# The last row's second layer norm from moments, in an adaLN, cached attention and token-mixing kernel

## The chip, the cores and the metric

The kernel runs on one core of a Trainium2 chip. The metric is the device time of one execution in microseconds (us); a run's time is given as the median of several executions. Each core has five engines with instruction queues of their own, each worked off in order: TensorE (PE in the profile, its weight loads PEld), VectorE (DVE), ScalarE (ACT), GpSimd (POOL) and SyncE (SP, which here issues nearly all DMAs).

## The reference

Four rows (batch B = 4, one token each, D = 512 channels), all arrays fp32. Cut to what matters:

```python
mod = (silu(c) @ w_mod).reshape(4, 6, 1, 512)       # sa, ca, ga, sb, cb, gb
h = layernorm(x) * (1 + ca) + sa
x = x + ga * attention(h, k_cache, v_cache, wq, wo) # 32 query heads, 8 kv heads, 4096 cached positions, head size 128
h = layernorm(x) * (1 + cb) + sb
# token mixing: a second layer norm of h, then one number per channel through an MLP of width 1792
n = layernorm(h)
u = gelu_tanh(n * w1 + b1)                          # (channel, 1792)
y = u @ w2 + b2                                     # one number per channel
out = x + gb * y
```

Each layer norm uses the variance over 512 channels with eps = 1e-5. The key and value caches are 2 MB for each of the 32 (row, kv head) pairs and kind, 128 MB in all; with the weights 157 MB are read.

## The kernel before

The 32 (row, head) pairs are numbered 0 to 31, eight of one row after another. Keys and values come in 4 MB loads (`load_pair`) into a ring of three slots, all on SyncE's queue. For each pair: `scores` (TensorE), the maximum over a row (`row_max`, `turn_max`, `col_max`, `spread_max`, `copy_max`), `expo` (ScalarE), `turn` (a transpose on VectorE), `values` (TensorE), `copy_v`, `pick`, `copy_o`, `project` (times wo) and `add_up`. The first 24 pairs run in a loop over `i`; the last eight follow a plan written out by hand, `PLAN`, a string of steps in which a letter names the operation and a number the pair: `V29` is `copy_v(29)`, `P28` is `add_up(28)`. The scheduler is manual: each engine executes its instructions in the order in which the program issues them.

While the pairs of row b + 1 run, the class `Mixer` does row b's modulation and mixing in small steps: `expand` (`x`, VectorE, two of the 14 chunks of the MLP width: u = hb * wr + b1 over all 512 channels), `gelu` (`g`, ScalarE, on such a chunk pair), `consume` (`c`, TensorE, contraction with w2 into the PSUM tile `py`). Row 2 is thus mixed during row 3's pairs, by the plan. Its last chunk pair is expanded into spare room of the slot that holds modulation 5 (`load_wm5`, step `LW`), and its last two pairs are contracted in the tail (`c c` in the last line of the plan), with `gather_up` (`zc`) copying `py` to SBUF on VectorE and folding it.

The channel layout: a [128, 128] tile holds row b of chunk c on the eight partitions from 32 * c + 8 * b, so 512 channels are four groups of partitions by 128 columns, and statistics over a row need a matmul across partitions.

Row 3, the last, has no pairs to hide behind. Its chain in the tail, after the last projection has filled `pgx[:, 4]` in PSUM and its mean was worked out ahead (`tally`, `mu`):

- `zs` (L741): ScalarE squares (x + mu) and sums along the columns; `zq` (L737): a matmul sums over the partitions.
- `za` (`centre`, L410): VectorE, a = (x + mu) * (1 + cb); `zx` (L747): a copy of x to `XK`.
- `zm` (`adaln_last`, L413): ScalarE's root sd (L416); h1 = sb * sd + a (L417), that is the modulated row times sd; terms that carry eps through the next norm (L419); its statistics `stats` (L378, L380).
- `T3` (L733): loads ScalarE's gelu tables with an activation of one element.
- `zb0`, `zb1` (`bcast`, L427): h1 spread over all partitions, two chunks of 128 channels each, into PSUM.
- `zv` (L479): the matmul that gathers the statistics; `zn` (`affine`): the aggregate (L396), hb = h1 - mean over all partitions in two halves on ScalarE (L436), the power -0.5 on GpSimd (`root`, L100) and wr = w1 * y (L437).
- `zw0` (L209): a quarter of modulation 5; then `finish` (L552): 14 chunks of expand, gelu and contract for the last row, closing and output.

Of the kernel before, what the change touches and what calls it, by code (L numbers as in the profile page):

```python
# [28 lines left out]
def adaln_decode(ctx: ExitStack, tc: tile.TileContext, small, x, wmod, wq, kk, kv, vv, wo, out):  # L29
# [47 lines left out]
    nc.gpsimd.memset(epsr[:, :, 2:3], EPS * 64)  # L77
    eps9 = cst.tile([P, 3], F32, name="eps9")
    nc.gpsimd.memset(eps9, 0.0)
    nc.gpsimd.memset(eps9[:, 0:1], 1e-20)  # L80
    nc.gpsimd.memset(eps9[:, 2:3], EPS * D)
    g32 = cst.tile([P, 32], F32, name="g32")
    dv.tensor_reduce(g32, ident.rearrange("p (c r) -> p r c", c=4), axis=AX.X, op=OP.add)
    eight = g32.rearrange("p (r x) -> p r x", x=8)[:, :, 0]
    sel4 = g32.rearrange("p (j r e) -> p j r e", j=4, e=2)[:, :, :, 0]
# [7 lines left out]
    prep = cst.tile([P, 4, P], F32, name="prep")  # L93
    osb = cst.tile([P, B, P], F32, name="osb")
    sT8 = cst.tile([P, 4, B, 8], F32, name="sT8")
# [63 lines left out]
    def slots():  # L159
        return ring.tile([P, 2, SK], F32, name="kv", tag="kv")  # L160
# [29 lines left out]
    def load_wm5():  # L190
        t = slots().rearrange("p s (k n) -> p (s k) n", n=D)
        nc.sync.dma_start(t[:, 0:4], wmod[2][:, 1])
        WM[5] = t[:, 0:4]
        return t[:, 4:6]

# [176 lines left out]

    XK = cst.tile([P, B, P], F32, name="xk")
    ZK = cst.tile([P, B - 1, P], F32, name="zk")
# [32 lines left out]

    def centre(x, mu):
        a = wk.tile([P, P], F32, name="a")
        dv.scalar_tensor_tensor(a, x, mu, prep[:, 3], op0=OP.add, op1=OP.mult)  # L410
        return a

    def adaln_last(b, pst, a):  # L413
        r = cst.tile([P, 1], F32, name="sd")
        h1 = wk.tile([P, P], F32, name="h1")
        nc.scalar.activation(r, pst, AF.Sqrt, bias=epsc, scale=1.0 / D)  # L416
        dv.scalar_tensor_tensor(h1, prep[:, 2], r, a, op0=OP.mult, op1=OP.add)  # L417
        pst = ps_m.tile([P, 27], F32, name="pst", tag="m")
        dv.tensor_scalar(pst[:, 24:27], eps9, r, r, op0=OP.mult, op1=OP.mult)  # L419
        return h1, stats(h1, b), pst  # L420

    def bcast(h1, b, pb=None, cs=range(4)):
# [26 lines left out]

    def contract_wide(py, u, js):  # L450
        for e, j in enumerate(js):
            q = j % 4
            mm(py[32 * q:32 * q + 32, :], w2[:, j:j + 1].to_broadcast([P, 32]), u[:, e, :],  # L453
               start=(j < 4), stop=(j >= NF - 4))

    class Mixer:
# [20 lines left out]

        def gather_more(self):
            mm(self.pst[:, 0:24], ones, self.st.rearrange("p a b -> p (a b)"), start=True, stop=True)  # L479
            self.st = self.pst  # L480

        def modulate(self):
            if self.b < B - 1:
                self.h1, self.st = adaln(self.b, self.st)
            else:
                self.h1, self.st, self.pst = adaln_last(self.b, self.st, self.a)

# [25 lines left out]
        def consume(self, most=9):  # L513
            if self.py is None:
                self.py = ps_e.tile([P, D if self.wide else P], F32, name="py", tag="e")
            for u, js in self.done[:most]:
                (contract_wide if self.wide else contract)(self.py, u, js)
            del self.done[:most]

        def gather_up(self):  # L520
            yw = wk.tile([P, D], F32, name="yw", tag="yw", bufs=1)
            dv.tensor_copy(yw, self.py)
            self.py = fold_groups(ps_e, yw, "e")

        def close(self):
# [25 lines left out]

    def finish(b, pg, py, hb, wr):  # L552
        uu = ring.tile([P, 16, D], F32, name="uu", tag="kv")
        for js in ((0,), (1,), (2, 3, 4), (5, 6, 7), (8, 9, 10), (11, 12), (13,)):
            j = js[0]
            if j < 2:
                nc.scalar.activation(uu[:, j], hb, AF.Gelu_apprx_tanh, bias=b1[:, j:j + 1], scale=wr[:, j:j + 1])
                u = uu[:, j:j + 1]
            else:
                u = uu[:, j:j + len(js)]  # L560
                expand(u, hb, wr, js)
                nc.scalar.activation(u, u, AF.Gelu_apprx_tanh)  # L562
            contract(py, u, js)
            if j == 1:
                modmm(pg, 5, (1, 2, 3))
        mix.close()
        dv.tensor_mul(osb[:, :B - 1], ZK, pg.unsqueeze(1).to_broadcast([P, B - 1, P]))
        dv.tensor_add(osb[:, :B - 1], osb[:, :B - 1], XK[:, :B - 1])
# [3 lines left out]
        dv.scalar_tensor_tensor(gx, gbl, b2, XK[:, b], op0=OP.mult, op1=OP.add)  # L572
# [23 lines left out]
    both = cst.tile([P, 2 * REP], F32, name="both")  # L596
    mu = cst.tile([P, 1], F32, name="mu")

    def tally_up():
# [18 lines left out]
    for i in range(NS - HKV):  # L618
# [30 lines left out]
        if i == 2:  # L649
            for t in range(2, 5):  # L650
                pm = mod(t)
                dst = prep[:, {2: 1, 3: 2, 4: 3}[t]]
                if t == 4:
                    dv.tensor_scalar(dst, pm, 1.0, None, op0=OP.add)
                else:
                    nc.scalar.activation(dst, pm, AF.Copy)
        if i == NS - HKV - 2:
            gate = spread_gate()

    mix, row = Mixer(B - 2), Mixer(B - 1)
    pve = pgx = pc = ep = spare = slot = None
    gates = list(range(2 * REP))
# [7 lines left out]
    LV28 L28 a27 g X30 t29.1 t29.0 l29 L29 s31 A27 LV29 b30 p27 x B30 S31 c c m31 e30 P27 X31 v28.0 f LT LV30  # L672
    b31 v28.1 B31 f e31 LV31 l30 V28 L30 t30.1 l31 L31 a28 t31.1 A28 p28 v29.0 v29.1 t30.0 f P28 V29 v30.0 a29
    v30.1 A29 LW p29 f v30.2 v30.3 t31.0 P29 g V30 Y y a30 A30 p30 E x v31.0 f v31.1 v31.2 v31.3 V31 z31 a31 I A31 j p31
    g T2 zs za zx zq c c zm zb0 T3 zv zb1 zw0 zn zc
    """
# [3 lines left out]
    MIX = {"F": mix.fold, "R": mix.residual, "G": mix.gather, "M": mix.modulate, "H": mix.gather, "Q": mix.spread,  # L680
           "N": mix.normalise, "g": mix.gelu, "c": lambda: mix.consume(1), "zc": mix.gather_up, "zv": row.gather_more,
           "zg": row.gather,
           "zm": row.modulate, "zn": lambda: row.normalise(cst.tile([P, 1], F32, name="yl"))}
    for step in PLAN.split():
# [25 lines left out]
        elif op == "LW":  # L710
            spare = load_wm5()
        elif op == "x":
            mix.expand(spare if mix.n == 6 else None)
        elif op == "f":
# [15 lines left out]
        elif step == "T2":  # L730
            nc.scalar.activation(tab, ones[0:1, 0:1], AF.Sqrt)
        elif step == "T3":
            nc.scalar.activation(tab, neg1, AF.Gelu_apprx_tanh)  # L733
        elif op == "zq":
            ph = ps_s.tile([P, 8, P], F32, name="ph3", tag="s")
            row.st = ph[:, 2, 0:1]
            mm(row.st, g32[:, 8 * (B - 1):8 * (B - 1) + 1].to_broadcast([P, P]), sq, start=True, stop=True)  # L737
        elif op == "zs":
            sq = cst.tile([P, 1], F32, name="sq")
            flat = wk.tile([P, P], F32, name="flat")  # L740
            nc.scalar.activation(flat, pgx[:, 4], AF.Square, bias=mu, accum_out=sq)  # L741
        elif op == "j":
            tally_up()
        elif op == "za":
            row.a = centre(pgx[:, 4], mu)
        elif op == "zx":
            dv.tensor_copy(XK[:, B - 1], pgx[:, 4])  # L747
        elif op == "zw":
            modmm(pgx[:, 0], 5, (0,))
        elif op == "zb":  # L750
            if i:
                py = ps_v.tile([P, 4, P], F32, name="py3", tag="pv")
            row.spread(py[:, 2:4] if i else ph[:, 4:6], (2 * i, 2 * i + 1))
    finish(B - 1, pgx[:, 0], py[:, 0], row.hb, row.wr)

# [33 lines left out]
```

## Time and profile before

| what | value |
| --- | --- |
| device time, median of 3 runs | 386.49 us (386.45 to 386.63) |
| span of the profiled execution, first to last instruction | 384.7 us |
| TensorE busy | 298.7 us (78%) |
| VectorE busy | 198.2 us (52%) |
| ScalarE busy | 112.2 us (29%) |
| GpSimd busy | 7.7 us (2%) |
| loads | 157.3 MB, q1 95.4% of the 16 DMA engines' span |

The profile gives the span of its execution; its own device time beside that is not listed, and the span lies 1.8 us under the median of the runs. A row of the timeline reads: start in us from the span's start, duration in us, engine, line, operation, output <- inputs, shapes, count, and in brackets how long the engine had been idle and what ended that.

### The profile page before, as it was taken

How to read it: one execution, taken by the hardware profiler on the slowest of the kernel's cores; microseconds unless marked ns; L12 is line 12 of the kernel's file. 1: busy time of each engine (PE TensorE's matmuls, PEld its weight loads, DVE VectorE, ACT ScalarE, POOL GpSimd, SP SyncE). 2: the span in 40 equal slices, each digit the busy share in tenths (PEclk: the TensorE clock that was granted, in tenths of full speed). 3: DMA queues.
4: the chain of work that ended last, by engine and by line, in shares of the span. 5: the costliest groups of instructions: out<-in, count | busy, mean ns of one | idle time of the engine just before them, and what ended most of it. 6: DMA issues, size and time to landing. Idle time of an engine off the chain costs nothing.

```text
span 384.7 us, 5604 instructions
## 1 busy us (share of the span) xinstructions
PE 298.7 (78%) x2380; PEld 117.2 (30%) x2380; DVE 198.2 (52%) x407; ACT 112.2 (29%) x144; POOL 7.7 (2%) x33
## 2 busy tenths in 40 slices
PE   0856777866966949979877878788888887999984
PEld 0112122311323313334322222342222343333653
DVE  1130251620451424664866545557665567778757
ACT  1001111121110110212567311124575105657276
POOL 1100000000000000000000000000000000000000
PEclk9989555985695685998999998999999999999999
DMA  8999999999999999999999999999999999999930
GB/s 331 433 433 436 411 453 433 409 432 436 423 441 433 434 436 436 434 436 431 429 425 433 428 433 434 429 433 431 429 434 436 434 436 432 424 417 423 418 122 3
DMA packets 7409, 157.69 MB, mean 410 GB/s; under 512 B 964, under 2 KB 1236, under 8 KB 1496
## 3 DMA queue, kind: packets, MB, share of 16 engines
q1 hardware_dynamic: 7376, 157.33, 95.4%
q8 instruction: 18, 0.29, 0.3%
q14 instruction: 7, 0.06, 0.0%
q10 hardware_dynamic: 8, 0.00, 0.0%
HBM read 157.32 MB, written 0.01 MB: 409 GB/s over the span
## 4 chain that ended last, share of the span: by engine, by line
DMA 60%; PE 29%; DVE 7%; ACT 2%; issue 1%; POOL 0%; SPq 0%; POOLq 0%; DVEq 0%
DMA kv<-in_kv 58%; PE s L231 8%; PE pv L291 7%; PE s L122 2%; PE qs L138 2%; DVE m L236 2%; DVE p L267 2%; DMA sm<-in_small 2%; PE pa L343 2%; PE pt L328 2%; ACT uu L562 1%; PE pb L251 1%; PE pve L303 1%; PE pm L240 1%; PE pgx L348 1%
## 5 line engine op out<-in xcount | busy, mean ns | idle before, releaser
L231 PE MATMUL s<-kv,QT 128*32 128x512 f32 x512 | 75.2, 714 | 38.9 <-DMA kv<-in_kv 37.0
L236 DVE TENSOR_REDUCE m<-s 128x1 f32<-128x1024 f32 x32 | 39.2, 1224 | 96.0 <-PE s L231 95.9
L261 ACT ACTIVATE p<-s,nm 128x1024 f32<-128x1024 f32 x32 | 35.7, 1115 | 180.6 <-DVE nm L256 180.5
L291 PE MATMUL pv<-kv,p 128*32 128x512 f32 x464 | 69.8, 670 | 0.7 <-DMA kv<-in_kv 0.7
L231 PEld LDWEIGHTS s<-kv,QT 128*32 128x32 f32 x512 | 15.8, 123 | 84.0 <-DMA kv<-in_kv 52.5
L328 PEld LDWEIGHTS pt<-g,po 128*128 128x128 f32 x236 | 31.1, 205 | 27.2 <-issue 19.9
L343 PE MATMUL pa<-wo,oT 128*32 128x512 f32 x240 | 34.6, 648 | 4.6 <-DVE oT L335 4.4
L328 PE MATMUL pt<-g,po 128*128 128x4 f32 (+2 forms) x236 | 33.9, 267 | 1.5 <-DVE po L314 1.0
L267 DVE STREAM_TRANSPOSE p<-p 128x1024 f32<-128x1024 f32 x25 | 30.9, 1234 | 0.0
L314 DVE COPY po<-pv 128x512 f32<-128x512 f32 x29 | 20.0, 688 | 16.8 <-PE pv L291 16.7
L245 DVE TENSOR_REDUCE mx<-pm 1x128 f32<-1x512 f32 x32 | 21.3, 669 | 1.1 <-PE pm L240 1.1
L442 DVE TENSOR_SCALAR u<-hb,wr,sm 128x512 f32<-128x512 f32 x40 | 19.9, 541 | 1.9 <-POOL wr L437 1.0
L506 ACT ACTIVATE u<-u 128x1024 f32<-128x1024 f32 x20 | 20.4, 1051 | 1.5 <-DVE u L442 1.4
L361 DVE TENSOR_TENSOR acc<-acc,pa 128x512 f32<-128x512 f32 x26 | 17.8, 686 | 4.3 <-PE pa L343 4.2
L261 ACT ACT_TABLE_LOAD x11 | 14.1, 1283 | 20.3 <-DVE nm L256 20.2
L251 PEld LDWEIGHTS pb<-neg,mx 1*128 1x128 f32 x64 | 10.4, 202 | 28.2 <-DVE mx L245 26.5
L122 PE MATMUL s<-wm,sT 128*4 128x512 f32 x16 | 9.1, 732 | 10.6 <-DVE sT L108 10.6
L506 ACT ACT_TABLE_LOAD x13 | 16.7, 1283 | 0.2
L291 PEld LDWEIGHTS pv<-kv,p 128*32 128x32 f32 x464 | 13.4, 146 | 7.2 <-issue 3.1
L240 PE MATMUL pm<-ident,m 128*1 128x128 f32 x32 | 9.3, 289 | 7.4 <-DVE m L236 3.5
L251 PE MATMUL pb<-neg,mx 1*128 1x1 f32 x64 | 13.1, 271 | 2.1 <-DVE mx L245 2.1
L453 PE MATMUL py<-u,sm 128*32 128x512 f32 x80 | 14.4, 616 | 0.0
(158 smaller groups left out, 214.7 us busy)
## 6 DMA issues: line engine op xcount, KB each, us to landing
kv<-in_kv SPq DMA_DIRECT2D x28, 4096.0 KB, 21.9
wq<-in_wq SPq DMA_DIRECT2D x2, 4096.0 KB, 16.3
wo<-in_wo SPq DMA_DIRECT2D x4, 2048.0 KB
kv<-in_kv SPq DMA_DIRECT2D x4, 2048.0 KB, 20.3
wm<-in_wmod SPq DMA_DIRECT2D x2, 2048.0 KB, 14.8
kv<-in_kk SPq DMA_DIRECT2D x1, 4096.0 KB
kv<-in_vv SPq DMA_DIRECT2D x3, 1024.0 KB
wm<-in_wmod SPq DMA_DIRECT2D x1, 1024.0 KB
```

Source lines behind the costliest of these rows:

```text
L231: mm(s[32 * c:32 * c + 32, n * 512:(n + 1) * 512], QT[:, b, h, :], KT[i][:, (n * 4 + c) * 512:(n * 4 + c + 1) * 512], start=True, stop=True)
L236: dv.tensor_reduce(M[i], S[i], axis=AX.X, op=OP.max)
L245: dv.tensor_reduce(mx, M[i].rearrange("o (c r) -> o r c", c=4).unsqueeze(1).to_broadcast([1, 4, 32, 4]), axis=AX.X, op=OP.max)
L251: mm(pb, M[i].rearrange("o c r -> o (c r)"), neg1, start=True, stop=True)
L261: nc.scalar.activation(p, S[i], AF.Exp, bias=M.pop(i), accum_out=l)
L267: dv.transpose(PL[i][0], PL[i][0])
L291: mm(PV[i][32 * q:32 * q + 32, :], pT[:, 128 * k:128 * k + 128:4], VT[i][:, 4 * k:4 * k + 4, :].rearrange("p j d -> p (j d)"), start=(k < ...
L314: dv.tensor_copy(PV[i], pv)
L328: mm(pt, po[:, c * DH:(c + 1) * DH], sel.unsqueeze(1).to_broadcast([P, m, REP]), start=(c == 0), stop=(c == n - 1))
L343: mm(pa[32 * g:32 * g + 32, :], oT[:, g:g + 1].to_broadcast([P, 32]), wo_t[h][:, g, :], start=True, stop=True)
L442: dv.tensor_scalar(u[:, e, :], hb, wr[:, j:j + 1], b1[:, j:j + 1], op0=OP.mult, op1=OP.add)
L506: nc.scalar.activation(u, u, AF.Gelu_apprx_tanh)
```

## The change

The last row's second variance is no longer taken from statistics of h1 but worked out from moments. With the shift sb centred beforehand (`spread_shift`, in the loop after pair 5, gives `spart` = sb minus its mean and sb's variance plus eps in `smv`), h1 = spart * sd + al, and the variance over the row times sd squared is E[al^2] + sd * E[2 al spart] + sd^2 * (var(sb) + eps) - (E[al])^2. The four sums along columns go into `mom`: ScalarE squares give the columns 0 and 2, VectorE's accumulators the columns 1 and 3; matmuls with constant columns 1/D and -1/D (`mid`, `nmid`) sum over partitions, each into a PSUM tile of its own (`row`, the tile of `first_moment`, and `ph[:, 0]`). Two small factors run on GpSimd (`kk1`), two on VectorE (`vv1`). The upper half of hb is written by VectorE, the lower by ScalarE. The copy of x to `XK` is gone; `gx` reads x from PSUM.

Row 2: the last `x` and its gelu, and the gelu before it, move ahead of `V29`; there `lift` (`zy`) copies the ten contracted chunks from `py` to SBUF on ScalarE. In the tail `fold_rest` (`zc`) folds that copy and contracts the last four chunks in narrow form. The output tile `osb` comes from the ring of `u` tiles.

```diff
-    eps9 = ...                                   # three memsets on GpSimd
+    mid = cst.tile([P, 1], F32, name="mid")
+    nc.gpsimd.tensor_scalar(mid, g32[:, 8 * (B - 1):8 * (B - 1) + 1], 1.0 / D, None, op0=OP.mult)
+    nmid = ...                                   # the same with -1.0 / D
...
-    def contract_wide(py, u, js):
+    def contract_wide(py, u, js, last):
...
-               start=(j < 4), stop=(j >= NF - 4))
+               start=(j < 4), stop=(last - 4 < j))
...
+        def lift(self):
+            self.yw = up.tile([P, 2, D], F32, name="u")[:, 0]
+            nc.scalar.activation(self.yw, self.py, AF.Copy)
+
+        def fold_rest(self):
+            py = ps_e.tile([P, P], F32, name="pc", tag="e")
+            for c in range(4):
+                mm(py[32 * c:32 * c + 32, :], g32, self.yw[:, c * P:(c + 1) * P], start=True, stop=False)
+            for u, js in self.done:
+                for e, j in enumerate(js):
+                    for c in range(4):
+                        mm(py[32 * c:32 * c + 32, :], w2[:, j:j + 1].to_broadcast([P, 32]),
+                           u[:, e, c * P:(c + 1) * P], start=False, stop=(j == NF - 1))
+            self.py = py
...
+    def spread_shift():                          # called in the loop where i == 5
+        psb = ps_m.tile([P, 4, P], F32, name="psb", tag="m")
+        for c in range(4):
+            e = 32 * c + 8 * (B - 1)
+            mm(psb[:, c, :], ident[:, e:e + 1].to_broadcast([P, P]), prep[:, 2], start=True, stop=True)
+        psb = psb.rearrange("p c n -> p (c n)")
+        st = wk.tile([P, 6], F32, name="st")
+        dv.bn_stats(st, psb)
+        dv.bn_aggr(smv, st)
+        dv.tensor_scalar(spart, prep[:, 2], smv[:, 0:1], None, op0=OP.subtract)
+        dv.tensor_scalar(smv[:, 1:2], smv[:, 1:2], EPS, None, op0=OP.add)
...
+    def last_rows(x):                            # za
+        al = wk.tile([P, P], F32, name="a")
+        flat = wk.tile([P, P], F32, name="flat")
+        dv.scalar_tensor_tensor(al, x, mu, prep[:, 3], op0=OP.add, op1=OP.mult, accum_out=mom[:, 1:2])
+        dv.tensor_tensor_reduce(flat, al, spart, 2.0, 0.0, OP.mult, OP.add, mom[:, 3:4])
+        return al
+    def squares(x, col, **kw):                   # zs (x + mu, column 0), zp (al, column 2)
+        flat = wk.tile([P, P], F32, name="sqr", tag="h1")
+        nc.scalar.activation(flat, x, AF.Square, accum_out=mom[:, col:col + 1], **kw)
+    def means(cols, dst=None, mid=mid):          # zq, zl, zv
+        if dst is None:
+            dst = ps_m.tile([P, 1], F32, name="pmo", tag="m")
+        mm(dst, mid.to_broadcast([P, P]), mom[:, cols], start=True, stop=True)
+        return dst
+    def first_root(g):                           # zk
+        nc.scalar.activation(sd, g, AF.Sqrt, bias=epsc)
+        nc.gpsimd.tensor_scalar(kk1[:, 0:1], sd, sd, smv[:, 1:2], op0=OP.mult, op1=OP.mult)
+    def modulate(al):                            # zh
+        h1 = wk.tile([P, P], F32, name="h1")
+        dv.scalar_tensor_tensor(h1, spart, sd, al, op0=OP.mult, op1=OP.add)
+        return h1
+    def first_moment(g):                         # zl
+        dv.tensor_copy(momc, g)
+        nc.gpsimd.tensor_scalar(kk1[:, 1:2], momc, momc, kk1[:, 0:1], op0=OP.mult, op1=OP.subtract)
+    def second_moments(g):                       # zm
+        dv.tensor_sub(vv1[:, 0:1], g[:, 0:1], kk1[:, 1:2])
+        dv.scalar_tensor_tensor(vv1[:, 1:2], g[:, 1:2], sd, vv1[:, 0:1], op0=OP.mult, op1=OP.add)
+    def affine_last(lo, hi):                     # zn
+        ...
+        root(vv1[:, 1:2], P, y)
+        nc.scalar.activation(hb[:, 0:D // 2], lo, AF.Identity, bias=momc)
+        dv.tensor_scalar(hb[:, D // 2:], hi, momc, None, op0=OP.add)
+        nc.gpsimd.tensor_tensor(wr, w1, y.to_broadcast([P, NF]), op=OP.mult)
...
-    f P28 V29 v30.0 a29
-    v30.1 A29 LW p29 f v30.2 v30.3 t31.0 P29 g V30 Y y a30 A30 p30 E x v31.0 f ... j p31
-    g T2 zs za zx zq c c zm zb0 T3 zv zb1 zw0 zn zc
+    f P28 g x g zy V29 v30.0 a29
+    v30.1 A29 LW p29 f v30.2 v30.3 t31.0 P29 V30 Y y a30 A30 p30 E v31.0 f ... j p31
+    T2 zs za zp zq zk T3 zl zh zv zm zb0 zb1 zn zw0 zc
```

More of the change, by code (lines that the diff above doesn't have):

```diff
@@ L656, in adaln_decode @@
                     nc.scalar.activation(dst, pm, AF.Copy)
+        if i == 5:
+            spread_shift()
         if i == NS - HKV - 2:
             gate = spread_gate()
-    mix, row = Mixer(B - 2), Mixer(B - 1)
-    pve = pgx = pc = ep = spare = slot = None
+    mix = Mixer(B - 2)
+    pve = pgx = pc = ep = slot = None
     gates = list(range(2 * REP))
@@ L680, in adaln_decode @@
     MIX = {"F": mix.fold, "R": mix.residual, "G": mix.gather, "M": mix.modulate, "H": mix.gather, "Q": mix.spread,
-           "N": mix.normalise, "g": mix.gelu, "c": lambda: mix.consume(1), "zc": mix.gather_up, "zv": row.gather_more,
-           "zg": row.gather,
-           "zm": row.modulate, "zn": lambda: row.normalise(cst.tile([P, 1], F32, name="yl"))}
+           "N": mix.normalise, "g": mix.gelu, "c": lambda: mix.consume(1), "zy": mix.lift, "zc": mix.fold_rest, }
     for step in PLAN.split():
@@ L710, in adaln_decode @@
         elif op == "LW":
-            spare = load_wm5()
+            load_wm5()
         elif op == "x":
-            mix.expand(spare if mix.n == 6 else None)
+            mix.expand()
         elif op == "f":
@@ L733, in adaln_decode @@
             nc.scalar.activation(tab, neg1, AF.Gelu_apprx_tanh)
-        elif op == "zq":
-            ph = ps_s.tile([P, 8, P], F32, name="ph3", tag="s")
[L736 to L741, printed above, removed]
+        elif op == "zs":
+            squares(pgx[:, 4], 0, bias=mu)
+        elif op == "za":
+            al = last_rows(pgx[:, 4])
+        elif op == "zp":
+            squares(al, 2)
+        elif op == "zq":
+            row = means(slice(0, 1))
+        elif op == "zk":
+            first_root(row[:, 0:1])
+        elif op == "zh":
+            h1 = modulate(al)
+        elif op == "zl":
+            first_moment(means(slice(1, 2), None, nmid))
+        elif op == "zv":
+            ph = ps_s.tile([P, 8, P], F32, name="ph3", tag="s")
+            means(slice(2, 4), ph[:, 0, 0:2])
+        elif op == "zn":
+            hb, wr = affine_last(*(t.rearrange("p c n -> p (c n)") for t in (ph[:, 4:6], py[:, 2:4])))
+        elif op == "zm":
+            second_moments(ph[:, 0, 0:2])
         elif op == "j":
             tally_up()
[L744 to L747, printed above, removed]
         elif op == "zw":
```

67 lines of the change are left out of this document (30 added, 37 removed).

## The prediction

> **What bounds the kernel now.** I read the chain that ended last first, then busy times by stretch, then the timeline of the last 25 us, engine by engine. The chain, as shares of the span by engine:
>
> ```profile
> DMA 60%; PE 29%; DVE 7%; ACT 2%; issue 1%; POOL 0%; SPq 0%; POOLq 0%; DVEq 0%
> ```
>
> Busy time by stretch near the end, columns named in its second line:
>
> ```profile
> core 0 of [0], span 384.7 us
> core 0: us, PE busy (x) PEld busy (x) DVE busy (x) ACT busy (x) POOL busy (x), PEclk, DMA share, GB/s
> 364.00:368.00 4.00, 3.64 (x98) 3.11 (x98) 2.64 (x10) 1.69 (x2) 0.00 (x0) 1.00 0.88 352
> 368.00:372.00 4.00, 3.42 (x59) 2.18 (x59) 1.91 (x10) 2.43 (x6) 0.00 (x0) 1.00 0.19 80
> 372.00:376.00 4.00, 2.89 (x54) 2.00 (x57) 3.06 (x8) 3.59 (x7) 0.76 (x2) 1.00 0.01 4
> ```
>
> The loads bound the span up to about 367 us. The last values are what TensorE waits for:
>
> ```profile
> 367.23 0.14 PEld L303 LDWEIGHTS pve<-kv,p 128*32 128x32 f32 x4 [0.17 <-DMA kv<-in_vv]
> ```
>
> Then 17.4 us of tail run with hardly a load: the last row's residual, statistics, modulation, second statistics, fourteen gelus, output. Most of the change lies there. The in-order queues of ScalarE, VectorE, TensorE and GpSimd, from the square of the last row to the gelus:
>
> ```profile
> 369.94 0.37 ACT L741 ACTIVATE flat<-pgx,mu 128x128 f32<-128x128 f32 x1 [1.07 <-PE pgx L348]
> 370.20 0.19 ACT L741 ACTIVATION_READ_ACCUMULATOR flat<-pgx,mu 128x1 f32 x1
> 370.87 0.26 ACT L416 ACTIVATE sd<-ph,epsc 128x1 f32<-128x1 f32 x1 [0.47 <-PE ph L737]
> 371.15 1.28 ACT L733 ACT_TABLE_LOAD   x1
> 372.44 0.20 ACT L733 ACTIVATE tab<-neg 1x1 f32<-1x1 f32 x1
> 372.96 0.47 ACT L436 ACTIVATE hb<-ph,mv 128x256 f32<-128x256 f32 x1 [0.31 <-DVE mv L396]
> 373.33 0.47 ACT L436 ACTIVATE hb<-py,mv 128x256 f32<-128x256 f32 x1
> 373.88 1.52 ACT L557 ACTIVATE uu<-hb,sm,wr 128x512 f32<-128x512 f32 x2
> 375.38 1.48 ACT L562 ACTIVATE uu<-uu 128x1536 f32<-128x1536 f32 x1
> ```
>
> ```profile
> 370.43 0.35 DVE L410 SCALAR_TENSOR_TENSOR a<-pgx,mu,prep 128x128 f32<-128x128 f32 x1 [0.77 <-ACT flat L741]
> 370.70 0.28 DVE L747 COPY xk<-pgx 128x128 f32<-128x128 f32 x1
> 371.16 0.35 DVE L417 SCALAR_TENSOR_TENSOR h<-prep,sd,a 128x128 f32<-128x128 f32 x1 [0.18 <-ACT sd L416]
> 371.43 0.28 DVE L419 TENSOR_SCALAR pst<-eps,sd 128x3 f32<-128x3 f32 x1
> 371.62 0.28 DVE L378 BATCH_NORM_STATS2 st<-h 128x6 f32<-128x128 f32 x1
> 371.94 0.18 DVE L380 TENSOR_TENSOR stm<-st,ident 128x24 f32<-128x24 f32 x1
> 372.64 0.28 DVE L396 BATCH_NORM_AGGREGATE mv<-pst 128x2 f32<-128x27 f32 x1 [0.52 <-PE pst L479]
> 372.84 0.63 DVE L522 COPY yw<-py 128x512 f32<-128x512 f32 x1
> 373.89 2.37 DVE L442 TENSOR_SCALAR uu<-hb,wr,sm 128x512 f32<-128x512 f32 x5 [0.42 <-POOL wr L437]
> ```
>
> ```profile
> 371.23 0.60 PE L453 MATMUL py<-kv,sm 128*32 128x512 f32 x2
> 371.75 0.71 PE L427 MATMUL ph<-h,ident 128*128 128x128 f32 x4
> 372.30 0.30 PE L479 MATMUL pst<-stm,ones 128*128 128x24 f32 x2
> 372.45 0.69 PE L427 MATMUL py<-h,ident 128*128 128x128 f32 x4
> ```
>
> ```profile
> 373.00 0.55 POOL L100 TENSOR_TENSOR yl<-mv,half 128x1 f32<-128x1 f32 x1 [54.02 <-DVE mv L396]
> 373.63 0.21 POOL L437 TENSOR_TENSOR wr<-w1n,yl 128x14 f32<-128x14 f32 x1
> ```
>
> From 373.88 ScalarE runs gelu on gelu without a gap, and the end follows at a fixed distance. So the question is when the first gelu of the last row starts. Now wr, ready at 373.84, starts it, after the chain square, root, h1, statistics, gather matmul, aggregate, power, product.
>
> **The change, part by part.**
>
> *Prologue.* Three memsets leave GpSimd and two 128x1 multiplies join. Between L437's 0.21 and L100's 0.55 each, they delay what follows on that queue by 0.1 to 0.8 us. I take 0, because the load queue is busy with the query weights then; without that cover it is this amount.
>
> *spread_shift after pair 5.* Eight passes like L427's (1.2 us at this clock), a 512-wide PSUM read (0.63 by L522), an aggregate (0.28) and two small operations: about 2.5 us, in front of the next pair. The cover:
>
> ```profile
> 143.25 1.08 PE L231 MATMUL s<-kv,QT 128*32 128x512 f32 x4 [5.20 <-DMA kv<-in_kv]
> ```
>
> TensorE waits 5.2 us for a load shortly after. Cost 0.
>
> *Row 2.* Its last expand, two gelus and a new copy to SBUF (lift) move ahead of copy V29 in the order. On VectorE that is between these two:
>
> ```profile
> 358.65 0.69 DVE L361 TENSOR_TENSOR acc<-acc,pa 128x512 f32<-128x512 f32 x1
> 360.40 0.29 DVE L314 COPY po<-pvn 128x128 f32<-128x128 f32 x1 [1.06 <-PE pvn L303]
> ```
>
> Two expands take 0.95 (five take 2.37) and fit the 1.06 idle, with some 0.1 to spare. Behind V29 wait pick, copy_o and project of pair 29 and the last values; the only later slack on that path is the 0.17 at the last load. The gelus and the lift run on ScalarE, which nothing else needs then. No DMA moves past another. In the tail the eight wide matmuls of 371.23 go, and fold_rest brings 8 + 32 narrow passes after the first part of modulation 5. Twelve such passes took this long:
>
> ```profile
> 364.71 0.53 PE L348 MATMUL pgx<-wo,both 128*32 128x128 f32 x12 [0.25 <-DVE both L335]
> ```
>
> So 40 take about 1.5 us. They begin near 373.4 and end near 374.9. The first contraction could start 0.8 us after the first gelu (L557: two in 1.52), at 374.4; it loses 0.5, which does not reach the end, since TensorE has only 8 + 8 + 24 more passes before the three-wide gelu ends near 376.6. Cost 0.
>
> *XK copy and output.* The 0.28 copy leaves VectorE, which then waited for the root anyway; gx reads PSUM, as L410 does in 0.35, the same as from SBUF. 0.
>
> *The tail, worked out.* Square and its accumulator end at 370.39, as now. The centring waits for the square now (0.77 <-ACT), and I keep that: 370.43 to 370.78. The new square of al comes ahead of the root on ScalarE. It has no per-partition bias; its price is this copy's:
>
> ```profile
> 36.12 0.28 ACT L155 ACTIVATE prep<-px 128x128 f32<-128x128 f32 x1
> ```
>
> 370.82 plus 0.28, and the accumulator's read overlapping 0.1: to 371.19. Root: 371.21 to 371.47, so 0.34 later than now. Behind it three ways run to the gelu:
> - ScalarE: table load to 372.77, warm-up to 372.97, lower half 0.47: 373.44, gelu at 373.5.
> - VectorE: h1 371.50 to 371.85. Then all eight broadcast passes without the statistics in between: now from 371.83 (end of L453) to 373.14, less 0.15 for L479, is 1.16, so 371.89 to 373.05. Upper half on VectorE: 0.28 at 128 columns and 0.63 at 512 give 0.40; with a scalar pointer I take 0.46, near ScalarE's 0.47. 373.09 to 373.55, gelu at **373.59**.
> - GpSimd: first factor from 371.55 (0.08 after its input, as at 373.00), second, then two VectorE operations of about 0.2 with hand-overs, power 0.55, product 0.21. A 128x1 multiply by pointer scalars has no row; its bounds are 0.21 (L437) and 0.55 (L100). I take 0.25, nearest to L437, also a multiply: factors done 372.13, variance 372.53, power 372.61 to 373.16, product 373.24 to 373.45, gelu at 373.5. At 0.21 it is 373.4, at 0.55 374.1.
>
> The latest decides: 373.59 against 373.88, a gain of **0.29 us**. Span 384.7 becomes 384.4. Only the span of the profiled execution is shown; the runs' median, 386.49, lies 1.8 above it, and I take the gain from the median: **386.2**.
>
> [...] GpSimd and VectorE overlap here now, in the same order of things as the first factor and h1 will:
>
> ```profile
> 314.57 0.38 DVE L404 SCALAR_TENSOR_TENSOR a<-xk,mv,prep 128x128 f32<-128x128 f32 x1
> ```
> ```profile
> 314.61 0.55 POOL L100 TENSOR_TENSOR ye<-mv,half 128x1 f32<-128x1 f32 x1 [55.49 <-DVE mv L396]
> ```
>
> GpSimd's power takes 0.55 beside a VectorE operation with two SBUF inputs, as it does at 373.00 beside one without, and VectorE 0.38 instead of 0.35. So I charge nothing. [...]
>
> **The rivals.**
> 1. *GpSimd decides.* Each 0.1 on a factor costs 0.2 on that way. Above 0.3 each it is the latest; above 0.44 each the kernel is slower than before: 386.7 at the 0.55 bound. Past 0.2% needs 0.83 each. For: pointer scalars are unpriced, and the power takes 0.55 for one column. Against: fourteen columns multiplied in 0.21. [...]
> 2. *The centring does not wait for the square*, since it is a different program: al at 369.95, its square behind the first one, root as now; the three ways start 0.34 earlier: 385.9. Against: both still read one PSUM tile, and L410 waits for ScalarE though it needs nothing of it.
> 3. *Slower: TensorE's granted clock falls* when the eight wide matmuls leave the middle of the tail. At half clock the 1.16 of broadcast passes becomes 2.3, and the gelu starts at 374.75: 387.4. It decides if the clock drops before 371.9. Against: TensorE is dense up to 370, and kept 1.00 in the stretch 372 to 376 with 2.89 of 4 us busy; about 2.5 remain.
> 4. *The tail's start moves.* The load stream lasts 365 us, and 0.2% of it is as much as all else; or the expand runs into V29. 385.4 to 386.9. Against: no byte and no load's order changes, and the runs shown lie within 0.18.
>
> **How the numbers follow.** What a measurement of this kernel can tell from no change is about 0.2%, 0.77 us. Forecast (VectorE's or ScalarE's way last, 386.0 to 386.45) 0.60; rival 1 (386.4 to 386.8) 0.15, of which 0.02 past the bound; rival 2 0.08, of which 0.02 below 385.72; rival 3 0.04; rival 4 0.13, of which 0.06 faster and 0.02 slower. Faster 0.08, slower 0.08, same 0.84. The range reaches down to 385.8, under rival 2's time, and up to 386.8, over rival 1's upper bound.
>
> **What would show it.** First gelu 0.2 to 0.4 us earlier against the end of the last values; the root some 0.3 later than now; the last three rows before the gelu those of VectorE's half; factors of 0.2 to 0.3 on GpSimd; broadcast passes in one block of 1.2 us; row 2's last gelus before 362 us and V29 not later than 360.5; a TensorE wait for a load at the last values as now. Wrong would be: factors over 0.44, a centring beside the square, a granted clock under 1.00 before 374, or last values off 367.2 by more than 0.3.

## The result, and the profile after

| | before | after |
| --- | --- | --- |
| device time, median of 5 runs | 386.49 us (386.41 to 386.63) | 388.55 us (388.26 to 389.75) |
| ratio, 95% interval | | 1.0057 (1.0045 to 1.0069) |
| span of the profiled execution | 384.7 | 387.9 (its own time: 389.75) |
| square of the last row to its first gelu | 3.94 | 4.87 |

The change costs 2.06 us where 0.29 us of gain was forecast. The profiled execution after is the slowest of the five; four have spans of 386.5 to 386.7. In it 2.26 us are lost ahead of the tail: the square starts at 372.20 instead of 369.94. TensorE's granted clock (third figure from the end) is low in one stretch there, first after, then before:

```profile
280.00:290.00 10.00, 9.77 (x45) 3.63 (x45) 3.88 (x6) 3.42 (x4) 0.00 (x0) 0.54 0.99 429
```
```profile
280.00:290.00 10.00, 7.96 (x65) 2.98 (x69) 6.51 (x12) 7.43 (x9) 0.00 (x0) 1.00 0.99 426
```

Another execution of the same kernel (again, below) has 1.00 in this stretch and the square at 369.96, so that part belongs to this one execution. The lag opens there: ScalarE's exponentials of one pair start at 277.63 here and 278.04 in again, those of the next pair at 290.39 and 286.35. That the clock caused it is not shown. From the first gelu to the end of the span it is 10.8 in both kernels. So the loss that both traced executions share lies between the square and the first gelu.

The timeline of after, from the square to the gelu:

```profile
372.20 0.37 ACT L623 ACTIVATE sqr<-pgx,mu 128x128 f32<-128x128 f32 x1 [6.16 <-PE pgx L346]
373.08 0.31 ACT L623 ACTIVATE sqr<-a 128x128 f32<-128x128 f32 x1 [0.43 <-DVE a L617]
373.39 0.24 ACT L632 ACTIVATE sd<-pmo,epsc 128x1 f32<-128x1 f32 x1
373.54 0.38 PE L628 MATMUL ph<-mom,mid 128*128 128x2 f32 x2
373.67 0.35 DVE L637 SCALAR_TENSOR_TENSOR h<-spart,sd,a 128x128 f32<-128x128 f32 x1
373.74 0.49 POOL L633 TENSOR_SCALAR kk<-sd,smv 128x1 f32<-128x1 f32 x1 [50.88 <-DVE momc L641]
374.33 0.39 POOL L642 TENSOR_SCALAR kk<-momc,kk 128x1 f32<-128x1 f32 x1
374.76 0.16 DVE L645 TENSOR_TENSOR vv<-ph,kk 128x1 f32<-128x1 f32 x1 [0.74 <-POOL kk L642]
374.95 0.22 DVE L646 SCALAR_TENSOR_TENSOR vv<-ph,sd,vv 128x1 f32<-128x1 f32 x1
375.22 0.71 PE L411 MATMUL ph<-h,ident 128*128 128x128 f32 x4 [1.30 <-DVE vv L646]
375.77 0.61 PE L411 MATMUL py<-h,ident 128*128 128x128 f32 x4
375.97 0.47 ACT L653 ACTIVATE hb<-ph,momc 128x256 f32<-128x256 f32 x1 [0.83 <-PE ph L411]
376.42 0.48 DVE L654 TENSOR_SCALAR hb<-py,momc 128x256 f32<-128x256 f32 x1 [1.25 <-PE py L411]
377.07 0.81 ACT L552 ACTIVATE uu<-hb,sm,wr 128x512 f32<-128x512 f32 x1 [0.62 <-DVE hb L654]
```

h1 (L637) is done at 374.02, but its broadcast (L411) starts at 375.22. The bracket names VectorE's second operation on the moments (L646), a value that the broadcast does not use. It does share the tile: the second moments lie in `ph[:, 0]`, which is not a tile of their own, since the lower half of the broadcast goes to `ph[:, 4:6]`. The operation ahead of L646 (L645) in turn waits for the two factors on GpSimd, 0.49 and 0.39.

Busy time by stretch, after:

```profile
core 0: us, PE busy (x) PEld busy (x) DVE busy (x) ACT busy (x) POOL busy (x), PEclk, DMA share, GB/s
374.00:375.20 1.20, 0.00 (x0) 0.00 (x0) 0.39 (x3) 1.13 (x2) 0.62 (x2) 1.00 0.00 0
375.20:376.20 1.00, 0.98 (x8) 0.97 (x8) 0.00 (x0) 0.23 (x1) 0.77 (x2) 1.00 0.00 0
376.20:378.20 2.00, 2.00 (x38) 1.88 (x40) 1.59 (x4) 1.38 (x3) 0.00 (x0) 0.54 0.05 12
```

TensorE (first pair of numbers) does nothing for 1.2 us, and about 1 us later its granted clock falls to half (0.54 as the mean of that stretch). That was too late to hurt the broadcast here.

### The profile page after: what moved, and what is told of

It reads as the page before. It is cut to its first block, busy times and chain, and to the rows that moved or that the text cites. A ratio compares the mean times of both kernels' runs of the same rounds, so it can differ in the third digit from the quotient of the medians.

```text
span 387.9 us, 5682 instructions
## 1 busy us (share of the span) xinstructions
PE 308.7 (80%) x2414; PEld 123.7 (32%) x2414; DVE 199.2 (51%) x412; ACT 112.6 (29%) x146; POOL 8.8 (2%) x34
## 4 chain that ended last, share of the span: by engine, by line
DMA 44%; PE 41%; DVE 11%; ACT 2%; POOL 1%; issue 1%; SPq 0%; ACTq 0%; POOLq 0%; DVEq 0%
DMA kv<-in_kv 42%; PE s L229 10%; PE pv L289 10%; PE pa L341 4%; PE pt L326 3%; DVE m L234 3%; DVE p L265 2%; PE s L121 2%; PE qs L137 2%; DMA sm<-in_small 2%; PE pb L249 2%; ACT uu L557 1%; PE py L437 1%; PE pm L238 1%; PE pve L301 1%
## 5 line engine op out<-in xcount | busy, mean ns | idle before, releaser
L229 PE MATMUL s<-kv,QT 128*32 128x512 f32 x512 | 76.8, 727 | 33.9 <-DMA kv<-in_kv 32.1
L289 PE MATMUL pv<-kv,p 128*32 128x512 f32 x464 | 72.5, 695 | 0.0
L326 PEld LDWEIGHTS pt<-g,po 128*128 128x128 f32 x236 | 32.8, 214 | 28.4 <-issue 18.7
L341 PE MATMUL pa<-wo,oT 128*32 128x512 f32 x240 | 37.0, 693 | 4.1 <-DVE oT L333 4.0
L326 PE MATMUL pt<-g,po 128*128 128x4 f32 (+2 forms) x236 | 35.5, 274 | 1.3 <-DVE po L312 0.8
L483 ACT ACTIVATE u<-u 128x1024 f32<-128x1024 f32 x21 | 21.4, 1052 | 3.8 <-DVE u L426 3.7
L426 DVE TENSOR_SCALAR u<-hb,wr,sm 128x512 f32<-128x512 f32 x42 | 20.9, 540 | 1.9 <-POOL wr L421 1.0
L238 PEld LDWEIGHTS pm<-ident,m 128*1 128x1 f32 x32 | 2.5, 79 | 38.3 <-DVE rl L278 27.4
```

The costliest lines, as they stand in the source:

```text
L229: mm(s[32 * c:32 * c + 32, n * 512:(n + 1) * 512], QT[:, b, h, :], KT[i][:, (n * 4 + c) * 512:(n * 4 + c + 1) * 512], start=True, stop=True)
L289: mm(PV[i][32 * q:32 * q + 32, :], pT[:, 128 * k:128 * k + 128:4], VT[i][:, 4 * k:4 * k + 4, :].rearrange("p j d -> p (j d)"), start=(k < ...
L326: mm(pt, po[:, c * DH:(c + 1) * DH], sel.unsqueeze(1).to_broadcast([P, m, REP]), start=(c == 0), stop=(c == n - 1))
L341: mm(pa[32 * g:32 * g + 32, :], oT[:, g:g + 1].to_broadcast([P, 32]), wo_t[h][:, g, :], start=True, stop=True)
L426: dv.tensor_scalar(u[:, e, :], hb, wr[:, j:j + 1], b1[:, j:j + 1], op0=OP.mult, op1=OP.add)
```

## The experiments

Two theories follow from this. *Tile*: the wait of the broadcast for VectorE's moments is the loss. *Clock*: TensorE, left idle in the tail, drops its clock in some executions and the broadcast takes longer (the forecast's rival 3). A third possibility was row 2's new order. In the table times are relative to the last row's square; the kernel before was timed at 386.43 to 386.46 beside each group.

| run | median us | ratio (95%) | broadcast starts | first gelu | span of that execution |
| --- | --- | --- | --- | --- | --- |
| before | 386.49 | | 1.81 | 3.94 | 384.7 |
| again | 388.27 | 1.0039 (1.0026 to 1.0052) | 3.03 | 5.78 | 386.5 |
| moments | 388.3 | 1.0056 (1.0044 to 1.0068) | 3.46 | 5.31 | 386.3 |
| row2 | 387.22 | 1.0017 (1.0009 to 1.0026) | 1.63 | 3.91 | 384.7 |
| own | 387.03 | 1.0021 (1.0002 to 1.0040) | 2.05 | 4.79 | 385.7 |
| row2_warm1 | 386.49 | 0.9995 (0.9982 to 1.0007) | 1.82 | 3.94 | 384.9 |
| own_half | 386.53 | 1.0001 (0.9981 to 1.0021) | 2.03 | 3.94 | 384.6 |
| after_half | 387.48 | 1.0022 (1.0012 to 1.0031) | 3.03 | 4.88 | 385.7 |
| dvef_half | 387.31 | 1.0019 (1.0010 to 1.0028) | 2.95 | 4.79 | 385.4 |
| best_half | 386.40 | 0.9991 (0.9981 to 1.0001) | 2.03 | 3.85 | 384.6 |
| best_k1 | 386.20 | 1.0001 (0.9987 to 1.0014) | 1.77 | 3.60 | 384.3 |
| best_none | 386.50 | 1.0007 (0.9998 to 1.0015) | 1.98 | 4.72 | 385.4 |

**The same kernel once more (again).**

> The changed kernel once more, for a second trace. Theory T (tail waits): the time from the last row's square to its first gelu is 4.9 us again (3.94 before), because that is fixed by waits; what varies is the start of the square, 372.2 in the first trace against 369.9 before, with TensorE's granted clock (0.50 from 240 to 250 and from 280 to 290 us there). With a mean clock of 0.88 to 0.91 the square starts near 371.0 and the time is 388.4. Rival R (row 2): the square starts 2 us or more late whatever the clock.

388.27 us, in two groups: two runs at 387.32 and 387.56, three at 388.27 to 388.33. The profiled one, of the upper group:

```profile
372.99 1.22 PE L411 MATMUL ph<-h,ident 128*128 128x128 f32 x4 [1.31 <-DVE vv L646]
373.99 1.06 PE L411 MATMUL py<-h,ident 128*128 128x128 f32 x4
375.09 0.48 DVE L654 TENSOR_SCALAR hb<-py,momc 128x256 f32<-128x256 f32 x1 [2.16 <-PE py L411]
375.74 0.81 ACT L552 ACTIVATE uu<-hb,sm,wr 128x512 f32<-128x512 f32 x1 [1.03 <-DVE hb L654]
```

```profile
core 0: us, PE busy (x) PEld busy (x) DVE busy (x) ACT busy (x) POOL busy (x), PEclk, DMA share, GB/s
371.76:372.96 1.20, 0.00 (x0) 0.00 (x0) 0.39 (x3) 1.13 (x2) 0.62 (x2) 1.00 0.00 0
372.96:373.96 1.00, 0.97 (x4) 0.97 (x5) 0.00 (x0) 0.00 (x0) 0.77 (x2) 0.54 0.00 0
```

The same wait, and this time the clock falls as soon as the broadcast begins (0.54 as the mean of that stretch): its eight passes take 2.06 (372.99 to 375.05) where after had 1.16. The gelu starts 5.78 after the square, 0.91 later than in the profile of after. So theory T met the time by luck: it had the square near 371.0 and 4.9 behind it. The upper group of again, and the spans of 386.5 to 386.7 of after, fit the square at 369.96 and a broadcast at half clock; only one of these executions was traced.

**New moments with row 2 in its old order (moments).** The plan's lines and `gather_up` go back to those of before; the tail reads `g T2 zs za zp zq c c zk T3 zl zh zv zm zb0 zb1 zn zw0 zc`.

> The new moments, factors and halves of hb, but row 2 in its old order (expand, gelus and the two wide contractions in the tail, copy on VectorE). Theory T: the tail's loss of 0.9 us stays, and what is lost before the tail stays too, since it has nothing to do with row 2: 388.0 to 388.6. Rival R: row 2's new order makes the tail start late; without it only the 0.9 of the tail is left, 387.4.

388.3 us. The wide contractions `c c` stand between `zq` and `zl` on TensorE, so the first moment comes later and the broadcast starts at 3.46. The moments carry the loss without row 2's order. That the time fell into the expected range is luck again: nothing is lost ahead of the tail (square at 369.81), and the tail loses 1.37 instead of 0.9.

**Row 2's order on the kernel before (row2 and, once more, row2_again).** The kernel before with the new plan lines for row 2, `lift` and `fold_rest`; the last norm as before.

> The kernel before with row 2's new order alone (last expand and two gelus ahead of V29, copy to SBUF by ScalarE, last four chunks contracted in narrow form). Theory T: same as before within 0.3, 386.2 to 386.8. Rival R: the tail starts about 1.1 later, 387.6.

> The kernel before with row 2 rearranged, a second look. Theory: if it is one of the slower executions (387.2-387.7), the granted clock falls to about half somewhere between 370 and 378, the eight passes of the broadcast or the work behind it take longer, and all before the tail stands as in the undisturbed look. Rival (row 2 itself is late): the square starts late at a full clock. At 386.5 it says nothing.

387.22 us, but the tail is that of before: square at 369.99, gelu at 3.91. Eight of its eleven spans are 384.5 to 384.8, like before, and three 385.3 to 385.5. What is more lies outside the span: 1.76 to 2.77 instead of 1.8, in row2_again 2.94 (387.64 with a span of 384.7). There the clock does fall, just behind the broadcast, and the end is not later:

```profile
374.02:376.02 2.00, 2.00 (x45) 1.98 (x40) 2.00 (x5) 2.00 (x3) 0.00 (x0) 0.50 0.07 16
```

So neither my theory (the clock) nor the rival (row 2 late) explains most of the 0.79 of this kernel (387.22 against 386.43); the three longer spans were not traced. No trace shows the time outside the span. The changed kernel does not have it: its five executions lie 1.76 to 1.88 over their spans.

**The second moments in a tile of their own (own).**

```diff
-            means(slice(2, 4), ph[:, 0, 0:2])
+            pm2 = ps_m.tile([P, 2], F32, name="pm2", tag="m")
+            means(slice(2, 4), pm2)
...
-            second_moments(ph[:, 0, 0:2])
+            second_moments(pm2)
```

> The changed kernel, but the two second moments in a PSUM tile of their own and not in the tile that the lower half of the broadcast goes to. Theory T: the broadcast passes then start right behind h1, 1.15 earlier, and GpSimd's way (factors 0.49 and 0.39, power, product) becomes the last: first gelu 0.8 to 0.9 earlier, 387.7. Rival: the wait for VectorE's second operation on the moments comes from something else (the queue, the factors); then nothing changes, 388.5.

387.03 us, half of the twelve runs at 386.41 to 386.76, five at 387.31 to 387.72, one at 391.02. In the trace (square at 370.12):

```profile
372.17 1.20 PE L411 MATMUL ph<-h,ident 128*128 128x128 f32 x4
```

The broadcast starts 2.05 after the square instead of 3.03, so the shared tile made that wait. In the profiled run (387.52) the passes took 2.06 again, at a clock of 0.50.

**Filler in TensorE's waits (row2_warm, own_warm, after_warm, best).** To test the clock without touching the chain, contractions that nobody reads:

```diff
+        elif op == "K":
+            dum = ps_e.tile([P, D], F32, name="dum", tag="e")
+            for q in range(4):
+                mm(dum[32 * q:32 * q + 32, :], w2[:, q:q + 1].to_broadcast([P, 32]), mix.yw, start=True, stop=True)
...
-    T2 zs za zp zq zk T3 zl zh zv zm zb0 zb1 zn zw0 zc
+    T2 zs K za zp zq zk T3 zl K zh zv zm zb0 zb1 zn zw0 zc
```

That is own_warm; after_warm has a third `K` behind `zv`, row2_warm `K K` in the place of before's `c c`.

> The kernel before with the new order of row 2, and eight 128x512 contractions whose result nobody reads at the place where the kernel before had its eight wide ones. Theory (TensorE's clock falls in the tail once this work is gone): the times close up around 386.4-386.5 again, with no group near 387.4, and the granted clock stays 1.00 from 370 to 378. Rival (the new order of row 2 costs time by itself, earlier): 387.2 and scattered as without the filler.

> The changed kernel with the second moments in a PSUM tile of their own, and four unread 128x512 contractions in each of TensorE's two waits (before the first square is summed, and after the first moment). Theory: no run with the clock at half, all near 386.4-386.5 (first gelu 3.95 after the square's start). Rival (the slow group comes from something else than TensorE's idle time): two groups again, 386.45 and 387.4.

> The changed kernel, its broadcast still behind the second moments, with four unread 128x512 contractions in each of three waits of TensorE in the tail. Theory: the wait on the second moments stays and the half clock goes: first gelu 4.85 after the square's start, 387.4 in nearly all runs. Rival A (the clock alone makes the loss): 386.4-386.6. Rival B (the filler does nothing): 387.4 and 388.3 as two groups.

> The filled kernel with the second moments' own tile, and two moves more: the second square goes behind the square root on ScalarE (the root 0.25 earlier), and both small factors are worked out on VectorE, behind the modulation. Theory: modulation 0.25 earlier, broadcast done at 3.15 after the square's start, upper half at 3.7, first gelu at 3.75 against 3.94 before: 386.2-386.3, below the kernel before. Rival (the second moments come too late behind the moved square, and GpSimd's root and the last scale decide): gelu 4.0 to 4.1, 386.5-386.6.

387.61, 386.89, 388.0 and 386.88 us; one of after_warm's twelve executions took 1421.41 us, and nothing on record says why. The clock stayed at 1.00 in the four tails up to 380 us. But I had taken a filler for half its length: it is eight matmul records and 1.04 to 1.06 us, as the whole `c c` of before, and it stood ahead of the broadcast (row2_warm: 2.98 after the square instead of 1.82). So the four were repeated with the right size: one `K` in row2_warm1, 256 columns in the others (`k`, eight records, 0.61 to 0.64).

**The fillers at their size (row2_warm1, own_half, after_half).**

> The kernel before with the new order of row 2 and four unread 128x512 contractions in the middle of the tail: eight matmul records there, as in the kernel before (the run with eight had sixteen, and its broadcast started 1.04 later). Theory (the new order of row 2 costs nothing, only the missing work does, through the clock): 386.4-386.5 in one group. Rival (row 2 costs by itself): 387.2 with the scatter of the run without filler.

> The second moments in their own PSUM tile, and unread contractions of 256 columns instead of 512 in TensorE's two waits, so that the filler takes 0.52 and no longer holds back the second moments. Theory: granted clock 1.00 through the tail, broadcast 2.2 after the square's start, first gelu 4.1 after it: 386.55-386.65, in one group. Rival (half the filler is too little for the clock): two groups, 386.5 and 387.4.

> The changed kernel, its broadcast still behind the second moments, with unread contractions of 256 columns in TensorE's three waits. Theory: the broadcast starts 3.05 after the square's start by the wait on VectorE's work on the moments, first gelu 4.9 after it: 387.4 in one group, 0.8 above the run with the tile of its own. Rival (the wait costs nothing at a full clock): as the run with the tile of its own.

386.49, 386.53 and 387.48 us, all within 0.1 of what was expected; after_half's twelve runs lie within 387.40 to 387.66, own_half's within 386.32 to 386.54 but for one at 390.84, and row2_warm1's within 386.38 to 386.68 but for one at 388.09. With the filler row 2 costs nothing, in time or in span. The broadcast and the gelu of after_half, by the timeline (square at 369.98):

```profile
373.01 0.71 PE L411 MATMUL ph<-h,ident 128*128 128x128 f32 x4 [0.29 <-DVE vv L646]
374.86 0.81 ACT L552 ACTIVATE uu<-hb,sm,wr 128x512 f32<-128x512 f32 x1 [0.62 <-DVE hb L654]
```

and of own_half, with GpSimd (square at 369.89):

```profile
371.36 0.35 DVE L637 SCALAR_TENSOR_TENSOR h<-spart,sd,a 128x128 f32<-128x128 f32 x1
371.44 0.49 POOL L633 TENSOR_SCALAR kk<-sd,smv 128x1 f32<-128x1 f32 x1 [50.99 <-DVE momc L641]
371.92 0.69 PE L411 MATMUL ph<-h,ident 128*128 128x128 f32 x4
372.03 0.39 POOL L642 TENSOR_SCALAR kk<-momc,kk 128x1 f32<-128x1 f32 x1
373.10 0.49 DVE L654 TENSOR_SCALAR hb<-py,momc 128x256 f32<-128x256 f32 x1 [0.23 <-PE py L411]
373.59 0.21 POOL L655 TENSOR_TENSOR wr<-sm,yl 128x14 f32<-128x14 f32 x1
373.83 1.52 ACT L552 ACTIVATE uu<-hb,sm,wr 128x512 f32<-128x512 f32 x2 [0.63 <-POOL wr L655]
```

The tile alone is worth 0.95 us (387.48 to 386.53); after_half's third filler ends at 372.72, ahead of its broadcast. With the shared tile gone, VectorE's half ends at 373.59 and GpSimd's last product at 373.80: GpSimd's way starts the gelu, 3.94 after the square, exactly as before the change.

**The factors on VectorE (dvef_half).** after_half with both factors on VectorE, issued behind h1.

> The changed kernel with the short filler and the second moments still in the broadcast's tile; only the two small factors move from GpSimd to VectorE, behind the modulation (0.27 each there). Theory (the broadcast waits for VectorE's work on the second moments, which waits for the factors): that work 0.35 to 0.4 earlier, the broadcast 2.7 after the square's start instead of 3.03, first gelu 4.55: 387.05-387.15, against 387.48 with the factors on GpSimd and 386.53 with the tile of its own. Rival (the factors do not matter, the shared tile alone does): 387.48.

387.31 us: 0.17 less than after_half, where 0.35 to 0.4 was expected.

```profile
371.61 0.27 DVE L641 TENSOR_SCALAR kk<-sd,smv 128x1 f32<-128x1 f32 x1
371.91 0.27 DVE L642 TENSOR_SCALAR kk<-momc,kk 128x1 f32<-128x1 f32 x1
372.76 0.71 PE L411 MATMUL ph<-h,ident 128*128 128x128 f32 x4 [0.22 <-DVE vv L646]
```

They are shorter there, but queue behind h1: the first starts 1.80 after the square (369.81) instead of 1.54 on GpSimd in after_half. The broadcast still waits for the moments; the engine of the factors is the small part.

**Towards a better version (best_half, best_k1, best_none).** Own tile, both factors on VectorE behind h1, and the second square issued behind the root: `T2 zs k za zq zk zp T3 zh zl k zv zm zb0 zb1 zn zw0 zc`. best_k1 keeps the first filler only, best_none neither.

> The second moments' own tile, the second square behind the root, both factors on VectorE behind the modulation, and the short filler. Theory: second moments summed 2.0 after the square's start, broadcast from 2.1, first gelu 3.85: 386.3-386.4, at or just below the kernel before. Rival (the last hand-over to the gelu and the upper half on VectorE take it back): 4.0 or more, 386.5-386.6.

> As the best version so far, without the second filler (between the first moment and the second moments); the first, ahead of the square's sum, stays. Theory: second moments summed and broadcast started 0.2 earlier, 1.8 after the square's start; first gelu 3.6: 386.15-386.2, faster than before by 0.25 to 0.3, if TensorE's waits that are left (0.3 and less) leave the clock up. Rival (the middle wait is the one that lowers the clock): 387.0 or two groups.

> The same without any filler. If TensorE's wait ahead of the square's sum (0.6) matters for the clock: two groups, 386.2 and 387.0 to 387.2. If the waits are now short enough: one group at 386.15-386.2, as with the first filler.

best_half: 386.40 us. best_k1: 386.20, nine of eleven runs at 386.08 to 386.37, two at 387.52 and 388.48; before beside it 386.46, 25 of 27 runs at 386.21 to 386.67. The interval holds 1, so that it is faster isn't shown; its span, 384.3 to 384.6 in those nine runs, and its gelu, 3.60 after the square (369.93), point to 0.3:

```profile
371.70 0.69 PE L411 MATMUL ph<-h,ident 128*128 128x128 f32 x4
372.88 0.48 DVE L654 TENSOR_SCALAR hb<-py,momc 128x256 f32<-128x256 f32 x1 [0.30 <-PE py L411]
373.29 0.21 POOL L655 TENSOR_TENSOR wr<-sm,yl 128x14 f32<-128x14 f32 x1
373.53 1.52 ACT L552 ACTIVATE uu<-hb,sm,wr 128x512 f32<-128x512 f32 x2 [0.25 <-POOL wr L655]
```

best_none, without the 0.61 of filler that stood ahead of the square's sum: 386.21 to 387.69, spread again, and in the profiled run (387.34) the clock falls before the broadcast:

```profile
core 0: us, PE busy (x) PEld busy (x) DVE busy (x) ACT busy (x) POOL busy (x), PEclk, DMA share, GB/s
369.70:370.45 0.75, 0.17 (x9) 0.04 (x1) 0.06 (x1) 0.46 (x2) 0.00 (x0) 1.00 0.00 0
370.45:371.70 1.25, 0.99 (x6) 0.82 (x6) 1.18 (x7) 0.85 (x4) 0.00 (x0) 0.78 0.00 0
371.70:372.90 1.20, 1.20 (x7) 1.20 (x8) 0.67 (x4) 1.18 (x2) 0.27 (x1) 0.50 0.00 0
```

The two kernels differ only in that filler. The other pairs say the same with more runs: own has six of twelve in its lower group and own_half eleven, again two of five and after_half all twelve. Up to 380 us, six of the eight traces without filler show half clock in the tail (after, again, moments, row2_again, own, best_none; not before and row2), and none of the ten with filler. That the filler keeps the clock up in the tail is read from these counts; in executions without a trace the clock is read from the time alone. The kernel before is not free of late executions either: 14 of the 120 beside these groups took 387.79 us or more, none of them traced.

The traces also tell something of why only some executions fall. In six of them (before, after, again, moments, row2, own) all changes of the clock from 230 us to the end of the span lie a multiple of 3.41 us apart. Cut at these moments, again and then after:

```profile
369.62:373.03 3.41, 1.46 (x19) 0.93 (x7) 1.59 (x9) 2.50 (x7) 0.90 (x3) 1.00 0.00 0
373.03:376.45 3.42, 3.42 (x36) 3.10 (x40) 1.16 (x3) 1.19 (x2) 0.75 (x2) 0.50 0.02 5
376.45:379.86 3.41, 2.80 (x92) 2.09 (x83) 3.41 (x8) 3.41 (x4) 0.00 (x0) 1.00 0.02 5
```
```profile
372.95:376.36 3.41, 2.04 (x18) 1.66 (x21) 1.27 (x8) 2.42 (x6) 1.65 (x4) 1.00 0.00 0
376.36:379.77 3.41, 3.41 (x69) 3.39 (x72) 3.16 (x7) 2.79 (x4) 0.00 (x0) 0.50 0.03 10
379.77:383.18 3.41, 2.63 (x88) 2.10 (x84) 3.31 (x9) 3.41 (x4) 0.00 (x0) 1.00 0.00 0
```

Where these moments fall against the tail differs between executions: the clock drops 3.07 after the square in again, 4.16 in after and 1.41 in own (371.53, back at 378.36). So again lost its broadcast to half clock and after, the same kernel, did not. That these moments decide it in general is argued from these traces, not tested. How much work in such a stretch keeps the clock up is not shown: TensorE was busy for 2.70 of the 3.41 us ahead of own's drop, and in before the clock stayed up after 2.06 (376.58 to 380.00).

## Why the prediction was wrong

The miss is 2.35 us (386.2 against 388.55). Between the square and the gelu of again, whose span is close to that of the median run, 2.13 of it can be found, in three steps; 0.22 stay unassigned:

| step | forecast | measured | runs |
| --- | --- | --- | --- |
| GpSimd's way ends last instead of VectorE's | 3.65 | 3.94 (+0.29) | own_half |
| the broadcast waits for the second moments | no wait | 4.88 (+0.94) | after_half against own_half |
| the clock falls before the broadcast | chance 0.04 | 5.78 (+0.90) | again against after_half |

- *VectorE's way, the step that failed.* "All eight broadcast passes without the statistics in between ... 371.89": the forecast had h1's end as the only thing that starts them. The diff puts the second moments into the broadcast's tile, and it also puts `zm`, which reads them, before `zb0`. I priced that reading for GpSimd's way, put the wait of the broadcast for it at nothing, and never asked who waits. It was 0.95 us in time (after_half against own_half). h1 itself was right: 1.82 after the square, forecast 1.91.
- *The factors.* 0.25 each leaned on the lower bound; 0.49 and 0.39 in after, 0.34 for the first in moments. Rival 1's break-even, 0.44 each, is what their mean turned out to be, and own_half came out even with before.
- *GpSimd beside VectorE.* I charged nothing for it. The first factor took 0.34 in moments, where VectorE was idle, and 0.49 beside h1 in own_half. A wait of the whole factor for h1's end would have given 371.71 plus 0.34, 372.05 in own_half, and it ended at 371.93. So it cost about 0.15, more than nothing and less than that wait; what makes the factor longer beside h1 is not shown.
- *Rival 3.* The mechanism, a broadcast at half clock, was right and the price near (0.90 measured, 1.16 said), the chance far too low: 0.04 was argued from the kernel before, whose tail is fuller. Row 2's wide matmuls were probably not only work moved, but helped to keep the clock up: the clock fell in row2_again, behind the broadcast, and not in before and row2_warm1, though not in the first trace of row2 either. And the wait on the tile emptied TensorE for another 1.2 us. In again the two losses are linked: the clock dropped 3.07 after the square, when the forecast had the broadcast all but done (3.11). Ahead of the fall TensorE's longest wait in the tail was 1.31 us in again and only 0.58 us in best_none. What sets the clock is not shown beyond its moments, multiples of 3.41 us apart from another start in each execution (the six traces above).
- *What held.* The square of al 0.31 (0.28 said), the root 0.24, the upper half on VectorE 0.48 (0.46 said), the broadcast at a full clock 1.16 (1.16 said). The centring still waits for the square (0.77), so rival 2 was void. The prologue and spread_shift cost nothing: in again the square starts at 369.96, before at 369.94. The tail's start (rival 4) moved in the one execution of after alone.
- *Row 2.* The rows of row2, around copy V29 on VectorE:

```profile
358.93 0.69 DVE L361 TENSOR_TENSOR acc<-acc,pa 128x512 f32<-128x512 f32 x1
359.54 1.00 DVE L442 TENSOR_SCALAR u<-hb,wr,sm 128x512 f32<-128x512 f32 x2
360.63 1.06 ACT L506 ACTIVATE u<-u 128x1024 f32<-128x1024 f32 x1 [2.31 <-DVE u L442]
360.68 0.29 DVE L314 COPY po<-pvn 128x128 f32<-128x128 f32 x1
```

V29 is at 360.68, past my bound of 360.5 and 0.28 later than before. But the addition ahead of it (L361) starts at 358.93, before at 358.65, so the 0.28 was there already, and from it to V29 it is 1.75 in both: the expand fits. The square starts at 369.99, so the tail did not wait for it either.

## What to carry to other kernels

Before charging a step by when its data is ready, list every earlier access to the tile that it writes: a small result parked in a free corner of a large PSUM tile can hold back the large write (0.95 us here, after_half against own_half). A matmul that looks like movable ballast may be what keeps TensorE's clock up (with 0.61 us of unread matmuls nine of best_k1's eleven runs lie within 386.08 to 386.37, without them best_none's spread over 386.21 to 387.69); when work leaves a latency-bound tail, ask what TensorE does in the waits that remain, and compare several executions. On this tail that filler decided more than the arithmetic saved: half clock in the broadcast cost 0.90 us (again against after_half), while the best gelu came 0.34 earlier than before the change (3.60 against 3.94).

## What was not expected of the hardware

- The granted clock fell to 0.5 after waits of TensorE of 0.58 to 1.31 us in a thin tail, in some executions only, at moments that lie multiples of 3.41 us apart and elsewhere in each execution; 0.61 us of unread matmuls ahead of the square's sum brought nine of eleven runs back to one group.
- A 128x1 multiply with two scalars from SBUF takes 0.34 to 0.49 us on GpSimd and 0.27 us on VectorE, more than GpSimd's product of 14 columns (0.21).
- The kernel before with row 2 rearranged took up to 1.1 us more outside its span, with the span unchanged (row2_again); with four unread matmuls more in the tail it was 1.74 to 1.89 (row2_warm1). Its cause stays open.
